# Two batches' k and v in 2304 B runs, block-diagonal exp(k), a t-outer first y and weight casts on GpSimd, in a linear-attention and GELU-MLP kernel

## The chip, the cores and the metric

The kernel runs on one core of a Trainium2 chip. The metric is the device time of one execution in microseconds (us); less is better. The kernel before takes 308.79 us (median of 3 runs, 308.36 to 309.51).

## The reference

Attention of the efficient kind (softmax of q over features, softmax of k over the sequence, then k'v, then q times that), and after it an MLP with an exact GELU. Inputs and output are float32.

```python
# q, k, v: (8 batches, 8 heads, 576, 64)
q_s = softmax(q, axis=-1)
k_s = softmax(k, axis=2)
kv  = einsum('bhsd,bhse->bhde', k_s, v)            # 64 x 64 per head
a   = einsum('bhsd,bhde->bhse', q_s, kv)
x   = a.transpose(0, 2, 1, 3).reshape(4608, 512)
out = gelu(x @ w_in) @ w_out                       # w_in 512 x 2048, w_out 2048 x 512
```

## The kernel before

Each batch of 576 rows is cut into 512 "main" rows and 64 "rest" rows; the rests of all batches are gathered into a ninth chunk. For a chunk, `h` is 16 tiles of four matmuls with a GELU on ACT behind each, and `y` is four groups (j) of 16 matmuls (t), each evacuated by DVE and stored. The attention of the next batch ("front") is woven into the matmuls. The parts that the argument touches:

```python
v_aug = [singles.tile([128, J, HP, PA], BF16, name=f"v_aug{i}") for i in range(2)]   # 4 x 4 x 130

def cast_v(b, hp):            # fp32 -> bf16, one pair of heads
    o = v_aug[b % 2][:, :, hp, :].rearrange("p j (two w) -> p two j w", two=2)
    s = st[b]["vf"].rearrange("p (x two) (j d) -> p x two j d", two=2, j=J)
    nc.vector.tensor_copy(out=o[:, :, :, 0:D], in_=s[:, hp])

def cast_v_all(b):
    cast_vr(b)                # the 64 rest rows
    for hp in range(HP):
        cast_v(b, hp)

def norm_q(b, parts=1, engs=None):       # later batches: reduce and reciprocal on DVE, multiply on GpSimd
    ...
        nc.vector.reduce_sum(out=qsum[:, :, hs], in_=eq[:, :, hs, :], axis=AX.X)
        nc.vector.reciprocal(recq[:, :, hs], qsum[:, :, hs])
        engs[i % len(engs)].tensor_tensor(out=eq[:, :, hs, :], in0=eq[:, :, hs, :], in1=..., op=ALU.mult)

def dve_front(b):
    norm_q(b)
    if b < B:
        cast_v_all(b)

def y_phase(c, ins):
    for j in range(J):
        ps = psum_y.tile([128, DM], FP32, tag="y")          # two banks in turn
        for t in range(NDF):
            nc.tensor.matmul(ps, g[:, t, j * 128:(j + 1) * 128], wo_bf[:, t, :], ...)
            for f in ins.get((j, t), []):
                f()
        y_sb = moe_sb.tile([128, DM], FP32, tag="y_sb")
        nc.vector.tensor_copy(out=y_sb, in_=ps)
        ...                                                  # store
...
for c in range(2, B + 1):
    ...
    h_phase(c, ins)                                          # c == 2: dve_front(3) in it
    if nb <= B:
        exp_q(nb) ... exp_k(nb); table(AF.Gelu)
        yi[(1, 15)] = [lambda nb=nb: dve_front(nb)]
    y_phase(c, yi)
```

The softmax here doesn't subtract the row's maximum and nothing guards it: scores larger than these inputs give would overflow.

## Time and profile before

| stage | from to (us) | length |
|---|---|---|
| start, to h of batch 0 | 0 to 21.24 | 21.24 |
| h of batch 0 | to 36.91 | 15.67 |
| y of batch 0, front of batch 1 | to 59.15 | 22.24 |
| h of batch 1 | to 74.67 | 15.52 |
| y of batch 1, front of batch 2 | to 93.16 | 18.49 |
| h of batch 2, front of batch 3 | to 109.87 | 16.71 |
| y of batch 2 | to 123.68 | 13.81 |

From there on h with a front (16.7) and y (13.8) alternate with no wait. A full group of 64 wide matmuls takes 13.81 us at full clock. A chain line has its start, its length and what ran; a timeline line adds the operation, shapes, count, and in brackets the idle time before it and what ended it.

The prediction does not show one place that later mattered: y of batch 2, on DVE and GpSimd. This is the timeline of the kernel before, of the two engines.

```profile
113.36 0.69 DVE L266 COPY y_sb<-ps 128x512 f32<-128x512 f32 x1 [2.76 <-PE ps L259]
114.08 2.29 DVE L159 TENSOR_REDUCE qsum<-e 128x32 f32<-128x2048 bf16 x1
116.40 0.35 DVE L160 RECIPROCAL recq<-qsum 128x32 f32<-128x32 f32 x1
116.67 0.36 DVE L136 CAST vr_aug<-r 64x512 bf16<-64x512 f32 x1
116.95 1.41 DVE L144 CAST v_aug<-f 128x512 bf16<-128x512 f32 x4
118.28 0.68 DVE L266 COPY y_sb<-ps 128x512 f32<-128x512 f32 x1
...
116.93 4.92 POOL L161 TENSOR_TENSOR e<-e,recq 128x2048 bf16<-128x2048 bf16 x1 [15.24 <-PE ps L259]
...
239.07 3.62 POOL L161 TENSOR_TENSOR e<-e,recq 128x2048 bf16<-128x2048 bf16 x1 [25.61 <-DVE recq L160]
```

Four casts of v follow one another every 0.35 us, the second evacuation of y comes right after them, and the GpSimd multiply (POOL), which was released at the same moment, takes 4.92 us beside them. The last line is the multiply of the ninth chunk, which has no casts of v beside it: 3.62 us.

### The profile page before, as it was taken

How to read it: one execution, taken by the hardware profiler on the slowest of the kernel's cores; microseconds unless marked ns; L12 is line 12 of the kernel's file. 1: busy time of each engine (PE TensorE's matmuls, PEld its weight loads, DVE VectorE, ACT ScalarE, POOL GpSimd, SP SyncE). 2: the span in 40 equal slices, each digit the busy share in tenths (PEclk: the TensorE clock that was granted, in tenths of full speed). 3: DMA queues.
4: the chain of work that ended last, by engine and by line, in shares of the span. 5: the costliest groups of instructions: out<-in, count | busy, mean ns of one | idle time of the engine just before them, and what ended most of it. 6: DMA issues, size and time to landing. Idle time of an engine off the chain costs nothing.

```text
span 307.6 us, 3824 instructions
## 1 busy us (share of the span) xinstructions
PE 288.6 (94%) x1541; PEld 138.4 (45%) x1541; DVE 122.0 (40%) x218; ACT 151.7 (49%) x212; POOL 38.3 (12%) x23
## 2 busy tenths in 40 slices
PE   5759998699899999999999999999999999999993
PEld 1424444244445544544454445444644455444441
DVE  4754437410777355342534344434433223110021
ACT  4546754367924582458245924591457056006400
POOL 6200002000204206000600060006000400000000
PEclk9588999699999999999999999999999999999999
DMA  7999999995026902691279117911600100110033
GB/s 219 316 381 387 369 263 304 312 304 152 2 102 190 286 23 84 188 271 51 73 207 270 37 69 213 265 36 68 153 21 34 70 34 0 36 70 33 2 68 68
DMA packets 47809, 46.38 MB, mean 151 GB/s; under 512 B 14000, under 2 KB 39600, under 8 KB 47792
## 3 DMA queue, kind: packets, MB, share of 16 engines
q1 hardware_dynamic: 47792, 46.14, 51.4%
q8 instruction: 12, 0.20, 0.3%
q14 instruction: 5, 0.04, 0.0%
HBM read 36.70 MB, written 9.44 MB: 150 GB/s over the span
## 4 chain that ended last, share of the span: by engine, by line
PE 89%; DVE 4%; ACT 3%; DMA 2%; issue 1%; POOL 1%; SPq 0%; ACTq 0%; DVEq 0%
PE ps L246 42%; PE ps L259 38%; PE ps L209 3%; PE ps L169 3%; PE ps L225 2%; DMA f<-in_q_dram 2%; ACT e L123 1%; DVE qsum L159 1%; PE ps L328 1%; DVE y_sb L266 1%; POOL e L161 1%; DVE xT L235 1%; PE ps L173 1%; DVE kvbd L197 0%; ACT L123 0%
## 5 line engine op out<-in xcount | busy, mean ns | idle before, releaser
L250 ACT ACTIVATE g<-ps 128x512 bf16<-128x512 f32 x144 | 86.0, 597 | 116.1 <-PE ps L246 116.1
L246 PE MATMUL ps<-xT,wi_bf 128*128 128x512 bf16 x576 | 136.5, 386 | 1.7 <-ACT wi_bf L294 1.7
L259 PE MATMUL ps<-wo_bf,g 128*128 128x512 bf16 x576 | 126.6, 379 | 1.2 <-DVE y_sb L266 1.2
L259 PEld LDWEIGHTS <-g 128*128 128x128 bf16 x576 | 56.3, 98 | 68.8 <-issue 1.9
L246 PEld LDWEIGHTS <-wi_bf 128*128 128x128 bf16 x576 | 55.9, 99 | 66.2 <-issue 4.7
L266 DVE COPY y_sb<-ps 128x512 f32<-128x512 f32 x36 | 24.8, 689 | 96.9 <-PE ps L259 96.9
L161 POOL TENSOR_TENSOR e<-e,recq 128x2048 bf16<-128x2048 bf16 (+1 forms) x9 | 33.9, 3765 | 203.8 <-DVE recq L160 171.4
L123 ACT ACTIVATE e<-f 128x2048 bf16<-128x2048 f32 (+1 forms) x20 | 31.2, 1563 | 7.9 <-DMA f<-in_q_dram 4.3
L235 DVE CAST xT<-ps 128x512 bf16<-128x512 f32 x32 | 21.8, 689 | 20.1 <-PE ps L225 16.8
L159 DVE TENSOR_REDUCE qsum<-e 128x16 f32<-128x1024 bf16 (+1 forms) x12 | 20.9, 1743 | 19.1 <-ACT e L123 18.9
L216 DVE COPY qT<-ps 128x1024 bf16<-128x1024 bf16 x17 | 11.6, 690 | 15.3 <-PE ps L209 15.3
L169 PE MATMUL ps<-v_aug,e 128*128 128x129 bf16 x128 | 11.7, 228 | 4.6 <-DVE v_aug L144 2.8
L209 PE MATMUL ps<-identity,e 128*128 128x128 bf16 x144 | 11.7, 229 | 4.0 <-POOL e L161 3.9
L169 PEld LDWEIGHTS <-e 128*128 128x128 bf16 x128 | 9.5, 101 | 9.9 <-DVE v_aug L144 2.6
L209 PEld LDWEIGHTS <-e 128*128 128x128 bf16 x144 | 9.9, 102 | 8.5 <-POOL e L161 5.0
L225 PE MATMUL ps<-qT,kvbd 128*128 128x512 bf16 x32 | 12.2, 401 | 1.5 <-ACT kvbd L193 1.2
L144 DVE CAST v_aug<-f 128x512 bf16<-128x512 f32 x32 | 11.7, 415 | 2.5 <-DMA f<-in_v_dram 2.5
L79 ACT ACT_TABLE_LOAD x9 | 11.5, 1283 | 0.9 <-PEq L439 0.7
L328 PE MATMUL ps<-zeros 128*128 128x512 bf16 x21 | 7.9, 528 | 1.2 <-DVE scr L69 1.2
L186 DVE RECIPROCAL rec<-ps 128x2 f32<-128x2 f32 (+1 forms) x18 | 3.0, 169 | 14.6 <-PE ps L173 14.6
L197 DVE TENSOR_TENSOR kvbd<-ps,rec 64x128 bf16<-64x128 f32 (+1 forms) x30 | 8.4, 278 | 0.9
L123 ACT ACT_TABLE_LOAD x6 | 7.7, 1283 | 0.1
(32 smaller groups left out, 63.1 us busy)
## 6 DMA issues: line engine op xcount, KB each, us to landing
out_dram<-y_sb SPq DMA_DIRECT2D x32, 256.0 KB, 2.3
f<-in_q_dram SPq DMA_DIRECT2D x6, 1024.0 KB, 7.5
f<-in_k_dram SPq DMA_DIRECT2D x6, 1024.0 KB, 10.5
f<-in_v_dram SPq DMA_DIRECT2D x6, 1024.0 KB, 10.2
w<-in_moe_w_out_dram SPq DMA_DIRECT2D x4, 1024.0 KB, 11.4
w<-in_moe_w_in_dram SPq DMA_DIRECT2D x3, 1024.0 KB, 11.1
f<-in_q_dram SPq DMA_DIRECT2D x4, 512.0 KB, 9.2
f<-in_k_dram SPq DMA_DIRECT2D x4, 512.0 KB, 8.9
```

The costliest lines, as they stand in the source:

```text
L123: nc.scalar.activation(out=dst[:, i * n:(i + 1) * n], in_=src[:, i * n:(i + 1) * n], func=AF.Exp)
L144: nc.vector.tensor_copy(out=o[:, :, :, 0:D], in_=s[:, hp])
L159: nc.vector.reduce_sum(out=qsum[:, :, hs], in_=eq[:, :, hs, :], axis=AX.X)
L161: engs[i % len(engs)].tensor_tensor(out=eq[:, :, hs, :], in0=eq[:, :, hs, :], in1=recq[:, :, hs].unsqueeze(3).to_broadcast([128, J, n, D]) ...
L169: nc.tensor.matmul(ps, st[b]["ek"][:, j, hs, :].rearrange("p h d -> p (h d)"), v_aug[b % 2][:, j, hp, 0:PW], start=(j == 0), stop=False,)
L209: nc.tensor.transpose(ps[:, j, i, :], st[b]["eq"][:, j, 2 * hp:2 * hp + 2, :].rearrange("p h d -> p (h d)"), identity,)
L225: nc.tensor.matmul(ps, kvbd[b][:, hp, :], st[b]["qT"][:, :, hp, :], start=True, stop=True)
L235: nc.vector.tensor_copy(out=st[b]["xT"][:, hp, :], in_=ps)
L246: nc.tensor.matmul(ps, wi_bf[:, dm, t * 128:(t + 1) * 128], xT[:, dm, :], start=(dm == 0), stop=(dm == NDM - 1),)
L250: nc.scalar.activation(out=g[:, t, :], in_=ps, func=AF.Gelu)
L259: nc.tensor.matmul(ps, g[:, t, j * 128:(j + 1) * 128], wo_bf[:, t, :], start=(t == 0), stop=(t == NDF - 1),)
L266: nc.vector.tensor_copy(out=y_sb, in_=ps)
```

## The change

Its intent is to shorten the start and the two transitions that are not hidden: load k and v of batches 0 and 1 in contiguous 2304 B runs (nine rows of a head per partition), use a block-diagonal exp(k) so that such runs serve as weights, cast weights on idle GpSimd, and let the first y run its first 48 matmuls over four banks before batch 1 is needed. Core of the diff, with cuts:

```diff
-    v_aug = [singles.tile([128, J, HP, PA], BF16, name=f"v_aug{i}") for i in range(2)]
+    v_flat = [singles.tile([128, HP * NS * VW], BF16, name=f"v_aug{i}") for i in range(2)]   # 4*9*66 = 2376
+    v_aug = [
+        t[:, 0:J * HP * PA].rearrange("p (j x w) -> p j x w", j=J, x=HP) for t in v_flat
+    ]
+    v_pair = [t.rearrange("p (x n w) -> p x n w", x=HP, n=NS) for t in v_flat]
...
+    def load_pair(b, name, t, parts):          # 2304 B runs
+        src = t[b].rearrange("h (p n) d -> (h p) (n d)", n=NS).rearrange("(x q) f -> q x f", q=128)
...
+    def exp_k_pair(b, half):                   # two ACT exps of 64 partitions each
...
+    def kv_pair(b, hp):                        # nine matmuls of 65 columns
...
-        for t in range(NDF):
-            ps = psum_h.tile([128, M], FP32, tag="h")
+        for t0 in [0] + list(range(group, NDF)):      # group=2: first two h tiles side by side
...
+            for h in range(2):                        # first two weight casts
+                nc.gpsimd.tensor_copy(out=o[:, 2 * h:2 * h + 2], in_=w[:, 2 * h:2 * h + 2, 0:n])
...
-    warm(12)
+    warm(24)
...
+    for t in range(12):                               # first y, over four banks
+        for j in range(J):
+            y_mm(0, yps[j], j, t)
+    norm_q(1, 0, 2)
+    norm_q(1, 1, 2)
+    cast_wo(3, wo[3])
...
+        (1, 12): [lambda: kv_step(2, (0, 1))],        # y of batch 1: finer places for batch 2's steps
+        (2, 2): [lambda: kv_step(2, (2, 3))],
...
-            yi[(1, 15)] = [lambda nb=nb: dve_front(nb)]
+            yi[(1, 0)] = [lambda nb=nb: norm_q(nb)]
+            if nb < B:
+                yi[(1, 15)] = [lambda nb=nb: cast_v_all(nb)]
```

Not shown: the v casts of batches 2 and 3 get a small memset of the ones column ahead of them. Batches 2 to 7 keep the old layout of v; for them `v_aug` is now a view into the first 2080 elements of the flat tile that batches 0 and 1 use as `v_pair`.

More of the change, by code (lines that the diff above doesn't have):

```diff
@@ L41 @@
     PA = 2 * D + 2
+    NS = S // 64
+    VW = D + 2
     singles = ctx.enter_context(tc.tile_pool(name="singles", bufs=1))
@@ L59 @@
     wo_bf = singles.tile([128, NDF, DM], BF16)
-    v_aug = [singles.tile([128, J, HP, PA], BF16, name=f"v_aug{i}") for i in range(2)]
+    v_flat = [singles.tile([128, HP * NS * VW], BF16, name=f"v_aug{i}") for i in range(2)]
[3 more added lines that the diff above has]
+    v_pair = [t.rearrange("p (x n w) -> p x n w", x=HP, n=NS) for t in v_flat]
+    ek_flat = [singles.tile([128, 2 * NS * 128], BF16, name=f"ek{i}") for i in range(2)]
+    ek_main = [
+        t[:, 0:J * H * D].rearrange("p (j h d) -> p j h d", j=J, h=H) for t in ek_flat
+    ]
+    ek_pair = [t.rearrange("p (x n m) -> p x n m", x=2, n=NS) for t in ek_flat]
     vr_aug = [singles.tile([128, HP, PA], BF16, name=f"vr_aug{i}") for i in range(2)]
@@ L70, in setup_tiles @@
         for i in range(2):
-            nc.vector.memset(v_aug[i][:, :, :, D:D + 1], 1.0)
+            nc.vector.memset(v_pair[i][:, :, :, D:D + 1], 1.0)
+            nc.vector.memset(ek_pair[i][0:64, :, :, 64:128], 0.0)
+            nc.vector.memset(ek_pair[i][64:128, :, :, 0:64], 0.0)
             nc.vector.memset(vr_aug[i][0:R, :, D:D + 1], 1.0)
@@ L74, in setup_tiles @@
             nc.vector.memset(ek_r[i][R:128], 0.0)
-        for b in range(B):
+        for b in range(B - 1):
             nc.gpsimd.memset(kvbd[b], 0.0)
@@ L81, with load_main @@
     st = [dict() for _ in range(B + 1)]
-    def load_main(b, name, t, eng, parts=1):
-        f = f32in.tile([128, H, J * D], FP32, tag=name + "f")
+    def load_main(b, name, t, parts=1):
+        f = f32in.tile([128, 2048 if name == "q" else 2560], FP32, tag=name + "f")
+        f = f[:, 0:2048].rearrange("p (h f) -> p h f", h=H)
         st[b][name + "f"] = f
@@ L88, in load_main, with load_both, load @@
         for i in range(parts):
-            eng.dma_start(out=f[:, i * n:(i + 1) * n, :], in_=src[:, i * n:(i + 1) * n, :])
-    def load_rest(b, name, t, eng):
-        r = f32in.tile([R, H, D], FP32, tag=name + "r")
-        st[b][name + "r"] = r
-        eng.dma_start(out=r, in_=t[b, :, M:S, :].rearrange("h p d -> p h d"))
-    def load(b, qp=1, kp=1, vp=1, keng=None):
-        keng = keng or nc.sync
-        load_main(b, "q", q, nc.sync, qp)
-        load_rest(b, "k", k, keng)
-        load_main(b, "k", k, keng, kp)
-        load_rest(b, "v", v, nc.sync)
-        load_main(b, "v", v, nc.sync, vp)
+            nc.sync.dma_start(out=f[:, i * n:(i + 1) * n, :], in_=src[:, i * n:(i + 1) * n, :])
+    def load_pair(b, name, t, parts):
+        f = f32in.tile([128, 2560], FP32, tag=name + "f")
+        f = f[:, 0:HP * NS * D].rearrange("p (x f) -> p x f", x=HP)
+        st[b][name + "f"] = f
+        src = t[b].rearrange("h (p n) d -> (h p) (n d)", n=NS).rearrange("(x q) f -> q x f", q=128)
+        n = HP // parts
+        for i in range(parts):
+            nc.sync.dma_start(out=f[:, i * n:(i + 1) * n, :], in_=src[:, i * n:(i + 1) * n, :])
+    def load_both(b, name, t):
+        f = f32in.tile([128, 2560], FP32, tag=name + "f")
+        r = f[0:R, 2048:2560].rearrange("p (h d) -> p h d", h=H)
+        f = f[:, 0:2048].rearrange("p (h f) -> p h f", h=H)
+        st[b][name + "f"], st[b][name + "r"] = f, r
+        nc.sync.dma_start(out=r, in_=t[b, :, M:S, :].rearrange("h p d -> p h d"))
+        nc.sync.dma_start(out=f, in_=t[b, :, 0:M, :].rearrange("h (p j) d -> p h (j d)", j=J))
+    def load(b):
+        load_main(b, "q", q)
+        load_both(b, "k", k)
+        load_both(b, "v", v)
     def load_qrest():
-        f = f32in.tile([128, J, H, D], FP32, tag="qf")
+        f = f32in.tile([128, 2048], FP32, tag="qf")
+        f = f.rearrange("p (j h d) -> p j h d", j=J, h=H)
         st[B]["qf"] = f
@@ L113, in exp_main @@
     def exp_main(b, name, parts=1):
-        e = attn_sb.tile([128, J, H, D], BF16, tag="e" + name)
+        if name == "q":
+            e = attn_sb.tile([128, J, H, D], BF16, tag="eq")
+        else:
+            e = ek_main[b % 2]
         st[b]["e" + name] = e
@@ L132, in exp_k, with cast_v_pair, norm_pair @@
         exp_main(b, "k", parts)
+    def exp_k_pair(b, half):
+        src = st[b]["kf"].rearrange("p x (n d) -> p x n d", n=NS)
+        for hh in range(2):
+            pr = slice(hh * 64, hh * 64 + 64)
+            nc.scalar.activation(
+                out=ek_pair[half][pr, :, :, hh * 64:hh * 64 + 64],
+                in_=src[pr, 2 * half:2 * half + 2], func=AF.Exp,
+            )
+    def cast_v_pair(b, hp, eng):
+        eng.tensor_copy(
+            out=v_pair[b][:, hp, :, 0:D],
+            in_=st[b]["vf"][:, hp, :].rearrange("p (n d) -> p n d", n=NS),
+        )
+    def kv_pair(b, hp):
+        ps = psum_a.tile([128, 512], FP32, tag="a")
+        st[b][f"kvp{hp}"] = ps
+        for n in range(NS):
+            nc.tensor.matmul(
+                ps[:, 0:D + 1], ek_pair[hp // 2][:, hp % 2, n, :], v_pair[b][:, hp, n, 0:D + 1],
+                start=(n == 0), stop=(n == NS - 1),
+            )
+    def norm_pair(b, hp, eng1):
+        ps = st[b][f"kvp{hp}"]
+        rec = small.tile([128, 2], FP32, tag="reck")
+        nc.vector.reciprocal(rec[:, 0:1], ps[:, D:D + 1])
+        for hh in range(2):
+            pr = slice(hh * 64, hh * 64 + 64)
+            dst = kvbd[b][pr, hp, hh * 64:hh * 64 + 64]
+            if hh == 1 and eng1 == "s":
+                nc.scalar.activation(out=dst, in_=ps[pr, 0:D], func=AF.Copy, scale=rec[pr, 0:1])
+            else:
+                nc.vector.tensor_scalar_mul(out=dst, in0=ps[pr, 0:D], scalar1=rec[pr, 0:1])
     def cast_vr(b):
@@ L146, in cast_v_all @@
     def cast_v_all(b):
+        if b < 4:
+            nc.vector.memset(v_aug[b % 2][:, :, :, D:D + 1], 1.0)
         cast_vr(b)
@@ L149, in cast_v_all, with norm_q @@
             cast_v(b, hp)
-    def norm_q(b, parts=1, engs=None):
-        engs = engs or [nc.gpsimd]
+    def norm_q(b, i=0, n=1, eng=None):
+        eng = eng or nc.gpsimd
         eq = st[b]["eq"]
-        qsum = small.tile([128, J, H], FP32, tag="qsum")
-        recq = small.tile([128, J, H], FP32, tag="recq")
-        n = H // parts
-        for i in range(parts):
-            hs = slice(i * n, (i + 1) * n)
-            nc.vector.reduce_sum(out=qsum[:, :, hs], in_=eq[:, :, hs, :], axis=AX.X)
-            nc.vector.reciprocal(recq[:, :, hs], qsum[:, :, hs])
-            engs[i % len(engs)].tensor_tensor(
-                out=eq[:, :, hs, :], in0=eq[:, :, hs, :],
-                in1=recq[:, :, hs].unsqueeze(3).to_broadcast([128, J, n, D]), op=ALU.mult,
-            )
+        w = H // n
+        hs = slice(i * w, (i + 1) * w)
+        qsum = small.tile([128, J, w], FP32, tag="qsum")
+        recq = small.tile([128, J, w], FP32, tag="recq")
+        nc.vector.reduce_sum(out=qsum, in_=eq[:, :, hs, :], axis=AX.X)
+        nc.vector.reciprocal(recq, qsum)
+        eng.tensor_tensor(
+            out=eq[:, :, hs, :], in0=eq[:, :, hs, :],
+            in1=recq.unsqueeze(3).to_broadcast([128, J, w, D]), op=ALU.mult,
+        )
     def kv_mm(b, ps, hp):
@@ L176, in kv_mm, with kv_step @@
         )
-    def kv_step(b, hps, split=False):
+    def kv_step(b, hps):
         n = len(hps)
@@ L190, in kv_step, with tp_mm @@
             dst = kvbd[b][pr, hx, hh * 64:hh * 64 + 64]
-            if split and hh == 1:
-                for i in range(n):
-                    nc.scalar.activation(
-                        out=dst[:, i], in_=src[:, i], func=AF.Copy, scale=rec[pr, i:i + 1]
-                    )
-            else:
-                nc.vector.tensor_tensor(
-                    out=dst, in0=src, in1=rec[pr, 0:n].unsqueeze(2).to_broadcast([64, n, D]),
-                    op=ALU.mult,
-                )
-    def tp_step(b, half, eng="v"):
+            nc.vector.tensor_tensor(
+                out=dst, in0=src, in1=rec[pr, 0:n].unsqueeze(2).to_broadcast([64, n, D]),
+                op=ALU.mult,
+            )
+    def tp_mm(b, half):
         if half == 0:
@@ L205, in tp_step @@
         ps = psum_a.tile([128, J, 2, 128], BF16, tag="a")
+        st[b][f"tp{half}"] = ps
         for i in range(2):
@@ L213, in tp_step, with tp_evac, x_mm @@
                 )
-        o = st[b]["qT"][:, :, 2 * half:2 * half + 2, :]
-        if eng == "v":
-            nc.vector.tensor_copy(out=o, in_=ps)
-        else:
-            nc.scalar.copy(out=o, in_=ps)
+    def tp_evac(b, half):
+        nc.vector.tensor_copy(
+            out=st[b]["qT"][:, :, 2 * half:2 * half + 2, :], in_=st[b][f"tp{half}"]
+        )
+    def tp_step(b, half):
+        tp_mm(b, half)
+        tp_evac(b, half)
     def x_step(b, hp, eng="v"):
+        x_mm(b, hp)
+        x_evac(b, hp, eng)
+    def x_mm(b, hp):
         if hp == 0:
@@ L223, in x_step @@
         ps = psum_a.tile([128, M], FP32, tag="a")
+        st[b][f"x{hp}"] = ps
         if b < B:
@@ L233, in x_step, with x_evac @@
                 )
+    def x_evac(b, hp, eng="v"):
+        ps = st[b][f"x{hp}"]
         if eng == "v":
@@ L237, in x_step, with h_phase @@
             nc.scalar.copy(out=st[b]["xT"][:, hp, :], in_=ps)
-    def h_phase(c, ins):
+    def h_phase(c, ins, group=1):
         g = moe_sb.tile([128, NDF, M], BF16, tag="g", bufs=1)
@@ L242, in h_phase, with y_mm, y_out @@
         xT = st[c]["xT"]
-        for t in range(NDF):
-            ps = psum_h.tile([128, M], FP32, tag="h")
+        for t0 in [0] + list(range(group, NDF)):
+            ts = range(t0, t0 + (group if t0 == 0 else 1))
+            pss = [psum_h.tile([128, M], FP32, tag="h", name="ps") for t in ts]
             for dm in range(NDM):
-                nc.tensor.matmul(
-                    ps, wi_bf[:, dm, t * 128:(t + 1) * 128], xT[:, dm, :],
-                    start=(dm == 0), stop=(dm == NDM - 1),
-                )
-            nc.scalar.activation(out=g[:, t, :], in_=ps, func=AF.Gelu)
-            for f in ins.get(t, []):
-                f()
+                for ps, t in zip(pss, ts):
+                    nc.tensor.matmul(
+                        ps, wi_bf[:, dm, t * 128:(t + 1) * 128], xT[:, dm, :],
+                        start=(dm == 0), stop=(dm == NDM - 1),
+                    )
+            for ps, t in zip(pss, ts):
+                nc.scalar.activation(out=g[:, t, :], in_=ps, func=AF.Gelu)
+                for f in ins.get(t, []):
+                    f()
+    def y_mm(c, ps, j, t):
+        nc.tensor.matmul(
+            ps, st[c]["g"][:, t, j * 128:(j + 1) * 128], wo_bf[:, t, :],
+            start=(t == 0), stop=(t == NDF - 1),
+        )
+    def y_out(c, ps, j):
+        y_sb = moe_sb.tile([128, DM], FP32, tag="y_sb")
+        last = c == B and j == J - 1
+        if last:
+            nc.vector.tensor_copy(out=y_sb[:, 0:DM // 2], in_=ps[:, 0:DM // 2])
+            nc.scalar.copy(out=y_sb[:, DM // 2:DM], in_=ps[:, DM // 2:DM])
+        else:
+            nc.vector.tensor_copy(out=y_sb, in_=ps)
+        if c < B:
+            dst = out[c * S:c * S + M, :].rearrange("(p j) n -> p j n", j=J)[:, j, :]
+            nc.sync.dma_start(out=dst, in_=y_sb)
+        else:
+            for b2 in range(2):
+                r0 = (2 * j + b2) * S + M
+                eng = nc.scalar if last and b2 == 1 else nc.sync
+                eng.dma_start(out=out[r0:r0 + R, :], in_=y_sb[b2 * R:(b2 + 1) * R, :])
     def y_phase(c, ins):
-        g = st[c]["g"]
         for j in range(J):
@@ L258, in y_phase @@
             for t in range(NDF):
-                nc.tensor.matmul(
-                    ps, g[:, t, j * 128:(j + 1) * 128], wo_bf[:, t, :],
-                    start=(t == 0), stop=(t == NDF - 1),
-                )
+                y_mm(c, ps, j, t)
                 for f in ins.get((j, t), []):
                     f()
-            y_sb = moe_sb.tile([128, DM], FP32, tag="y_sb")
-            nc.vector.tensor_copy(out=y_sb, in_=ps)
-            if c < B:
-                dst = out[c * S:c * S + M, :].rearrange("(p j) n -> p j n", j=J)[:, j, :]
-                nc.sync.dma_start(out=dst, in_=y_sb)
-            else:
-                for b2 in range(2):
-                    r0 = (2 * j + b2) * S + M
-                    nc.sync.dma_start(out=out[r0:r0 + R, :], in_=y_sb[b2 * R:(b2 + 1) * R, :])
+            y_out(c, ps, j)
     wi_cols = [256, 256, 512, 512, 512]
@@ L290, in cast_wi @@
         o = wi_bf[:, :, wi_off[i]:wi_off[i] + n]
-        if eng == "v":
+        if eng == "p":
+            for h in range(2):
+                nc.gpsimd.tensor_copy(out=o[:, 2 * h:2 * h + 2], in_=w[:, 2 * h:2 * h + 2, 0:n])
+        else:
             nc.vector.tensor_copy(out=o, in_=w[:, :, 0:n])
-        else:
-            nc.scalar.copy(out=o, in_=w[:, :, 0:n])
     def load_wo(i):
@@ L304, in cast_wo @@
         nc.vector.tensor_copy(out=wo_bf[:, 4 * i:4 * i + 4, :], in_=w)
-    def kv_chain(b, warm=lambda n: None):
-        cast_vr(b)
-        cast_v(b, 0)
-        cast_v(b, 1)
-        kv_step(b, (0, 1), split=True)
-        warm(2)
-        cast_v(b, 2)
-        kv_step(b, (2,), split=True)
-        x_step(b, 0)
-        x_step(b, 1, "s")
-        warm(2)
-        cast_v(b, 3)
-        kv_step(b, (3,), split=True)
-        x_step(b, 2)
-        x_step(b, 3, "s")
-    zeros = singles.tile([128, 512], BF16)
+    zeros = kvbd[B - 1].rearrange("p x m -> p (x m)")
     def warm(n):
@@ L328, in warm @@
             nc.tensor.matmul(ps, zeros[:, 0:128], zeros, start=True, stop=True)
-    load(0, qp=2, kp=2, vp=4)
+    load_main(0, "q", q, 2)
+    load_pair(0, "k", k, 2)
+    load_pair(0, "v", v, 4)
     wi = [load_wi(i) for i in range(5)]
-    wo = [load_wo(i) for i in range(4)]
-    load(1, qp=2, kp=2, vp=4)
+    wo = [load_wo(i) for i in range(3)]
+    load_main(1, "q", q, 2)
+    wo.append(load_wo(3))
+    load_pair(1, "k", k, 2)
+    load_pair(1, "v", v, 4)
     load(2)
@@ L337 @@
     setup_tiles()
-    warm(12)
+    warm(24)
     table(AF.Exp)
     exp_q(0, parts=2)
-    exp_k(0, parts=2)
-    table(AF.Gelu)
-    norm_q(0, parts=2, engs=[nc.gpsimd, nc.vector])
-    tp_step(0, 0)
-    tp_step(0, 1)
-    warm(5)
-    kv_chain(0, warm)
-    cast_wi(0, wi[0], "s")
-    cast_wi(1, wi[1], "v")
+    exp_k_pair(0, 0)
+    exp_k_pair(0, 1)
+    norm_q(0, 0, 2)
+    norm_q(0, 1, 2)
+    tp_step(0, 0)
+    cast_v_pair(0, 0, nc.vector)
+    cast_v_pair(0, 1, nc.gpsimd)
+    kv_pair(0, 0)
+    tp_mm(0, 1)
+    norm_pair(0, 0, "s")
+    table(AF.Gelu)
+    cast_v_pair(0, 2, nc.vector)
+    tp_evac(0, 1)
+    kv_pair(0, 1)
+    warm(2)
+    norm_pair(0, 1, "s")
+    x_step(0, 0)
+    cast_v_pair(0, 3, nc.gpsimd)
+    kv_pair(0, 2)
+    norm_pair(0, 2, "s")
+    x_step(0, 1, "s")
+    kv_pair(0, 3)
+    norm_pair(0, 3, "s")
+    x_step(0, 2)
+    x_step(0, 3, "s")
+    cast_wi(0, wi[0], "p")
+    cast_wi(1, wi[1], "p")
     cast_wi(2, wi[2], "v")
@@ L355 @@
         12: [lambda: cast_wo(1, wo[1])],
-    })
+    }, group=2)
     exp_q(1, parts=2)
-    exp_k(1, parts=2)
+    exp_k_pair(1, 0)
+    exp_k_pair(1, 1)
     table(AF.Gelu)
     cast_wo(2, wo[2])
-    cast_wo(3, wo[3])
-    y_phase(0, {
-        (2, 0): [lambda: norm_q(1, parts=2, engs=[nc.gpsimd, nc.vector])],
-        (3, 3): [lambda: tp_step(1, 0)],
-        (3, 7): [lambda: tp_step(1, 1, "s")],
-    })
-    kv_chain(1)
-    h_phase(1, {12: [lambda: cast_v_all(2)]})
+    yps = [psum_h.tile([128, DM], FP32, tag="h", name="ps") for j in range(2)]
@@ new lines @@
+    yps += [psum_y.tile([128, DM], FP32, tag="y", name="ps") for j in range(2)]
+    for t in range(12):
[3 more added lines that the diff above has]
+    norm_q(1, 1, 2)
+    cast_wo(3, wo[3])
+    tp_step(1, 0)
+    for t in range(12, NDF):
+        y_mm(0, yps[0], 0, t)
+    y_out(0, yps[0], 0)
+    for t in range(12, NDF):
+        y_mm(0, yps[1], 1, t)
+    tp_step(1, 1)
+    y_out(0, yps[1], 1)
+    for t in range(12, NDF):
+        y_mm(0, yps[2], 2, t)
@@ new lines @@
+    cast_v_pair(1, 0, nc.gpsimd)
+    cast_v_pair(1, 1, nc.vector)
+    kv_pair(1, 0)
+    norm_pair(1, 0, "v")
+    for t in range(12, NDF):
+        y_mm(0, yps[3], 3, t)
+    kv_pair(1, 1)
+    x_step(1, 0)
+    cast_v_pair(1, 2, nc.gpsimd)
+    norm_pair(1, 1, "v")
+    cast_v_pair(1, 3, nc.vector)
+    kv_pair(1, 2)
+    x_step(1, 1, "s")
+    norm_pair(1, 2, "v")
+    kv_pair(1, 3)
+    norm_pair(1, 3, "v")
+    x_step(1, 2)
+    x_step(1, 3, "s")
+    y_out(0, yps[2], 2)
+    y_out(0, yps[3], 3)
@@ L372 @@
+    h_phase(1, {12: [lambda: cast_v_all(2)]}, group=2)
     load(3)
-    exp_q(2)
+    exp_q(2, parts=2)
     exp_k(2)
-    def front3():
-        exp_q(3)
-        exp_k(3)
-        table(AF.Gelu)
-    front3()
-    y_phase(1, {
-        (0, 15): [lambda: norm_q(2, parts=2, engs=[nc.gpsimd, nc.vector])],
-        (1, 15): [lambda: kv_step(2, (0, 1)), lambda: kv_step(2, (2, 3))],
-        (2, 7): [lambda: tp_step(2, 0), lambda: tp_step(2, 1)],
-        (3, 3): [lambda hp=hp: x_step(2, hp, "v") for hp in range(HP)],
+    exp_q(3)
@@ L387 @@
+    exp_k(3)
+    table(AF.Gelu)
+    y_phase(1, {
+        (0, 15): [lambda: norm_q(2, 0, 2)],
+        (1, 1): [lambda: norm_q(2, 1, 2, nc.vector)],
+        (1, 12): [lambda: kv_step(2, (0, 1))],
+        (2, 2): [lambda: kv_step(2, (2, 3))],
+        (2, 4): [lambda: tp_step(2, 0)],
+        (2, 6): [lambda: tp_step(2, 1)],
+        (3, 0): [lambda: x_step(2, 0)],
+        (3, 4): [lambda: x_step(2, 1)],
+        (3, 8): [lambda: x_step(2, 2)],
+        (3, 12): [lambda: x_step(2, 3)],
     })
```

## The prediction

> **What bounds the kernel now.** I read the page's header and its 40 slices first, then the chain that ended last in order of time, to see where the tensor engine (PE) is not in its steady rhythm; then busy time by stage; then the timeline of the stages that the change touches. PE is busy for 94% of the span, so the share alone says little. The slices say where it is not at full rate:
>
> ```profile
> PE   5759998699899999999999999999999999999993
> PEclk9588999699999999999999999999999999999999
> DMA  7999999995026902691279117911600100110033
> ```
>
> One slice is 7.69 us. PE has gaps in slices 0 to 2, around 7 and at 10. The granted clock is low in slices 1 to 3 and at 7. DMA is saturated for the first nine slices and not later. From slice 12 on there is nothing to win: the chain shows each group of 64 wide matmuls at 13.81 us, with no wait until the last copy.
>
> ```profile
> 0.00:21.24 21.24, 12.35 (x62) 6.05 (x62) 12.79 (x32) 11.17 (x16) 6.33 (x15) 0.84 0.97 298
> 21.24:36.91 15.67, 15.67 (x65) 6.77 (x66) 6.64 (x6) 8.96 (x15) 0.00 (x0) 0.89 1.05 383
> 36.91:59.15 22.24, 18.42 (x106) 8.82 (x104) 13.47 (x25) 10.83 (x15) 1.90 (x1) 0.92 1.13 288
> 59.15:74.67 15.52, 15.52 (x66) 6.63 (x64) 1.51 (x5) 9.54 (x17) 0.00 (x0) 0.90 0.99 281
> ```
>
> These are stages: window and its length, busy time of PE, weight loads, DVE, ACT, POOL, then granted clock, DMA share and GB/s. The two h stages (second and fourth line) cost 15.67 and 15.52 us instead of 13.81 and show a clock near 0.9: each starts cold. The third line is y of batch 0 with the front of batch 1: 22.24 us.
>
> The chain shows what the head of the program hangs on:
>
> ```profile
> 16.74 0.59 DVE xT L235
> 17.34 0.35 DVE v_aug L144
> ...
> 18.43 0.23 DVE kvbd L197
> ...
> 18.74 0.32 ACT kvbd L193
> ...
> 19.10 0.40 PE ps L225
> ...
> 19.53 0.58 ACT xT L237
> ...
> 20.14 1.05 ACT wi_bf L294
> ...
> 21.24 3.02 PE ps L246 x7
> ```
>
> Columns are start, us, what. DVE casts, reciprocals and scalings alternate with short PE pieces, and the weight cast on ACT comes last: 1.7 us between the last xT matmul (19.5) and h. The same ladder stands between y and h of batch 1 (51.73 to 59.15). Before y of batch 1 ends there is one more hole:
>
> ```profile
> 78.52 1.23 DVE qsum L159
> ...
> 80.02 1.09 DVE qsum L159
> ...
> 81.56 1.54 issue
> 83.10 0.69 DVE y_sb L266
> ...
> 83.83 1.89 PE ps L259 x8
> ```
>
> The evacuation of y stands behind both reductions and a multiply on DVE; PE waits 1.16 us for it.
>
> **What the Trainium skill says.** (1) "TensorE: Matmul & The Clock Gate", Part 1, What's actually happening: after about one idle window of 3.4 us PE runs at half clock, and needs a busy window to recover. The trace agrees: the first four h matmuls take 1.71 us instead of 0.86, until about 25.0, 3.8 us after 21.24. (2) "SBUF — State Buffer", Who interferes with whom: DVE casts in a two-port mode, and DVE operations with two SBUF inputs against a reading GpSimd operation, exclude GpSimd for a whole instruction. It fits: the DVE multiply of 1024 elements takes 1.41 to 1.72 us when it starts under a POOL multiply, against 1.22 for the DVE reduction of the same size. (3) "ScalarE: Activation LUTs", What ACT_TABLE_LOAD costs: 186 ns plus 0.833 ns per element. The trace has 1056 ns for 1024 elements and 618 for 512, on 64 partitions: elements per partition count, so half the partitions save nothing. (4) "DMA: Bandwidth & Descriptors", Specifications: at least 512 B for line rate. The trace is stricter: weights in 2 KB runs land 1.05 MB every 2.71 us (387 GB/s; casts start at 20.51, 23.22, 25.93), q halves in 1 KB runs 0.52 MB in 1.69 us (310), and the 256 B rest of k 0.13 MB in about 1.46 us (90).
>
> **The change part by part.**
>
> *k and v in 2304 B runs.* I take 387 GB/s for them. q still lands at 6.4. Then k halves (0.59 MB, 1.52 us each) at 7.9 and 9.4, v quarters (0.76 us) at 10.2, 10.9, 11.7, 12.5, where before k ended at 11.0 and the second v quarter came at 13.3. All later loads move up by about 2 us; batch 1's q moves another 2.7 ahead of one weight load.
>
> *Block-diagonal exp(k).* Four ACT exps of 1152 elements (186 + 960 = 1.15 us, about 1.06 apart), against 0.63 + 2 x 1.06 = 2.75: about 1.5 us more ACT work per batch. Ready at 10.1 (first half) and 12.2 (second), against 12.08 before, so nothing is lost at the end and the first half comes 2 us earlier. On PE nine matmuls of 65 columns replace five of 129 per pair; the trace's 0.057 us per kv matmul warm, 0.107 cold, is the weight load's pace, so 0.51 against 0.29: +0.9 us warm per batch.
>
> *Start to h of batch 0.* Transposes at 9.4 as before (POOL multiply 7.43 to 9.33). The second multiply moves from DVE to POOL, 9.33 to 11.23. The first DVE v cast is ready to go at 10.7 but shares the port with it, so it ends at 11.7. kv 0 at 11.75 to 12.8, cold; norm to 13.75 (DVE, then ACT, as in the chain); the table load then holds ACT to 15.2; second transposes to 13.6, kv 1 to 14.6, its norm ends on ACT at 15.6. x0 at 15.2, kv 2, x1 at 16.0, kv 3 at 16.3 to 16.75, norm 2 to 17.05, x2 at 17.1, xT1 on ACT to 17.6, norm 3 to 17.9, x3 at 17.95. h begins at 18.2, against 21.24. Side by side, h has six matmuls (1.3 us) before it needs xT3 (18.85), so that copy is hidden. The weight casts on POOL (four pieces of 512 elements; the trace has no such POOL copy; my estimate is 0.7 us each from its two-input 1.9 us per 1024) run from about 14.4 to 17.8: off the path. Saved: 3.0 us.
>
> *Clock in h of batch 0.* PE now works without a long pause from 11.75 on. If it stays warm, h takes 13.81: 1.86 saved. I give that 65%: 1.2 us.
>
> *y of batch 0 and front of batch 1.* With h starting at 18.2, y starts at 32.0. t outer: 48 matmuls, 10.4 us, to 42.4, which need neither wo 3 nor batch 1. wo 3 lands near 38.5; its cast waits for the POOL multiplies (to 40.5) and ends at 41.7: just in time. Then transposes 0.45, two y (0.86 each), transposes, y, kv 0 (0.5), y: 47.4. What is left is a DVE ladder: kvbd 0 at 47.7, xT0 to 48.9, norm 1 to 49.6, v cast to 50.05, norm 2 to 50.75, norm 3 to 51.5, then x3 and h at 51.75. So 19.75 us from h to h, against 22.24: 2.5 saved. The second h probably still starts cold: PE does about 1.9 us in 3.4 before it; I put 40% on warm, worth 1.7: 0.7.
>
> *y of batch 1.* PE now does 13.81 + kv 1.15 + transposes 0.89 + x 0.88 = 16.7 against 18.49 (74.67 to 93.16): the y evacuation no longer stands behind both reductions. Taken as 1.6.
>
> *End.* The last copy is split (0.69 to about 0.42) and one of two stores is issued from ACT. After the copy ends at 303.56 the program runs 4.0 us more, for two issues in a row and a landing of 2.3. Estimate 0.6.
>
> Sum: 3.0 + 1.2 + 2.5 + 0.7 + 1.6 + 0.6 = 9.6. A schedule laid by hand has no slips; I take 0.6 off for those: 9.0 us, 308.8 to 299.8 us.
>
> **Rivals.** (a) Clock: the gain in PE's order is real, but both h stages start cold; then 1.9 of the sum goes: 301.7. For: both did before, and the gate's window is not tied to the program. Against: the long gap before h (18.4 to 21.2) goes. If both stay warm: 298. (b) The shared port and the single ACT become the bound of the start: POOL now has multiplies, v casts and weight casts, and ACT's 4.3 us of exp plus a table load lie between the norms. If POOL's copies take 1.5 us instead of 0.7, or DVE and POOL block each other at each cast, h starts at 20 or so: 301.5 to 302.5. For: 1.41 and 1.72 us for a 1.22 us operation. (c) Nothing is gained from the loads by themselves, because after 12.5 the ladder and not the data sets the pace; then undoing the run length alone would cost 1 to 2 us, at the start only. (d) t outer stalls for wo 3 or for g; slack is only 0.7 us, so a stall of 1 to 2 us is possible: 301.5.
>
> **Range and chances.** The warm-warm case with no slip gives 296.8; cold-cold with one of (b) or (d) gives 303.2. That is my 8 in 10. Two per cent faster is 302.6: it needs 6.2 of my 9.0 us. I put 0.82 on faster, 0.17 on same and 0.01 on slower.
>
> **What would show it.** h of batch 0 starts at 18.2 (within 1), lasts about 13.8 if warm; y's first 48 matmuls have no gap; h of batch 1 starts near 52; the 1.16 us hole in y of batch 1 is gone; from h of batch 2 on each stage is as before. POOL copies over 1.2 us, DVE casts of 576 elements far over 0.46 us, or a clock near 0.9 in both h stages would make it wrong.

## The result, and the profile after

Median 321.23 us (319.89 to 322.09, 4 runs) against 308.69 (308.36 to 309.51, 4 runs). The ratio is 1.0398, 95% interval 1.0354 to 1.0443: slower. A ratio here is the mean time of one kernel's fast runs over that of the other's fast runs of the same rounds, so it is not quite the ratio of the medians.

The page's slices of the changed kernel (one slice is 7.97 us):

```profile
PE   8599997999959969999799969996999999999994
PEclk9799997999989997999799979999999999999999
```

The start is fuller than before and its clock higher. But PE has new dips at slices 11, 14, 19, 23 and 27, where the kernel before showed nines, and the clock dips at or just after four of them (11, 15, 19, 23). The stages of the changed kernel, as windows (columns as in the prediction; two of the stages are told in the text only):

```profile
0.00:17.33 17.33, 12.05 (x83) 6.50 (x84) 12.23 (x32) 11.55 (x15) 11.41 (x21) 0.90 0.91 316
17.33:31.14 13.81, 13.81 (x65) 6.24 (x64) 5.59 (x5) 9.43 (x16) 0.00 (x0) 1.00 1.04 385
...
67.10:84.10 17.00, 16.93 (x106) 8.61 (x105) 11.35 (x21) 11.81 (x11) 1.90 (x1) 1.00 0.24 82
84.10:106.04 21.94, 18.26 (x105) 9.54 (x104) 13.53 (x21) 9.13 (x16) 3.98 (x1) 0.92 0.64 168
106.04:124.17 18.13, 15.66 (x66) 6.70 (x64) 10.40 (x11) 7.42 (x7) 3.91 (x1) 0.91 0.12 44
```

The first five stages came out much as predicted: h of batch 0 starts at 17.33 instead of 21.24 (saved 3.91) and is warm (13.81, saved 1.86); the next stage takes 20.45 against 22.24 (1.79); h of batch 1 is cold as before (15.51, clock 0.89); y of batch 1 takes 17.00 against 18.49 (1.49). With 0.34 at the end (4.39 us from the last matmul to the end, against 4.73) that is 9.4 us saved. Then it is lost: h of batch 2 takes 5.23 more, and y of batches 2 to 5 take 4.32, 4.39, 4.08 and 2.70 more. That is 20.7 us, and 20.7 less 9.4 is the 11.3 us by which the span grew (318.9 against 307.6).

The chain of the changed kernel shows y of batch 2:

```profile
112.58 0.35 DVE recq L228
112.93 0.28 DVE vr_aug L202
113.20 0.34 DVE v_aug L210
113.57 3.73 DVE v_aug L210
117.33 0.44 DVE v_aug L210
118.13 0.69 DVE y_sb L345
118.87 5.30 PE ps L333 x16
```

and the timeline of the changed kernel has GpSimd beside it, and PE:

```profile
113.10 3.91 POOL L229 TENSOR_TENSOR e<-e,recq 128x2048 bf16<-128x2048 bf16 x1 [21.40 <-PE ps L333]
...
118.87 5.30 PE L333 MATMUL ps<-wo_bf,g 128*128 128x512 bf16 x16 [2.46 <-DVE y_sb L345]
```

DVE does the same instructions in the same order as before, and the multiply starts at the same point (0.17 us after the reciprocal's end, 0.18 before). But the second v cast takes 3.73 us instead of 0.41 and ends at 117.30, 0.29 us after the multiply; the multiply takes 3.91 instead of 4.92. The second evacuation of y stands behind the casts, so the fourth y group waits 2.46 us for its bank, and then its 16 matmuls take 5.30 us instead of 3.45 (a quarter of 13.81) because PE went cold: the granted clock from 118.87 to 124.17 is 0.68. Of the 4.3 us, 2.5 are wait and 1.85 clock.

The list of DVE's instructions in the two built programs (not a profile) shows the one difference at that place. Before, and then after:

```
108 L144 TensorCopy v_aug0_91<-f_877 128x2x4x64 x3
114 L210 TensorCopy v_aug0_91<-f_916 128x2x4x64 [waits DVE_49] x3
```

In the changed program the second to fourth v cast of batches 2 to 6 each wait on DVE's own semaphore, that is for DVE's previous instruction to be complete (in batches 2 and 3 the first one too, behind its memset). Below this is called a self-wait.

### The profile page after: what moved, and what is told of

The parts are those of the page before. It is cut to its first block, busy times and chain, and to the rows that moved or that the text cites. A ratio compares the mean times of both kernels' runs of the same rounds, so it can differ in the third digit from the quotient of the medians.

```text
span 318.9 us, 3908 instructions
## 1 busy us (share of the span) xinstructions
PE 292.7 (92%) x1578; PEld 140.2 (44%) x1578; DVE 140.2 (44%) x224; ACT 152.9 (48%) x210; POOL 42.6 (13%) x32
## 4 chain that ended last, share of the span: by engine, by line
PE 76%; DVE 18%; issue 2%; ACT 2%; POOL 1%; DVEq 0%; ACTq 0%; POOLq 0%
PE ps L323 38%; PE ps L333 30%; DVE v_aug L210 7%; DVE qsum L227 4%; PE ps L272 3%; DVE y_sb L345 2%; PE ps L296 2%; PE ps L237 2%; DVE kvbd L198 1%; DVE v_aug L174 1%; POOL e L229 1%; ACT ek L152 1%; DVE recq L228 1%; PE ps L241 0%; DVE qT L279 0%
## 5 line engine op out<-in xcount | busy, mean ns | idle before, releaser
L333 PE MATMUL ps<-wo_bf,g 128*128 128x512 bf16 x576 | 133.0, 389 | 10.0 <-DVE y_sb L345 10.0
L345 DVE COPY y_sb<-ps 128x512 f32<-128x512 f32 x35 | 23.6, 686 | 88.4 <-PE ps L333 88.4
L309 DVE CAST xT<-ps 128x512 bf16<-128x512 f32 x32 | 22.1, 691 | 21.6 <-PE ps L296 18.2
L210 DVE CAST v_aug<-f 128x512 bf16<-128x512 f32 x24 | 26.7, 1112 | 3.1 <-DMA f<-in_v_dram 2.4
L279 DVE COPY qT<-ps 128x1024 bf16<-128x1024 bf16 x18 | 12.4, 691 | 18.4 <-PE ps L272 18.2
L152 ACT ACTIVATE e<-f 128x1024 bf16<-128x1024 f32 (+1 forms) x11 | 15.8, 1442 | 4.8 <-DMA f<-in_q_dram 4.7
L272 PEld LDWEIGHTS <-e 128*128 128x128 bf16 x144 | 9.8, 101 | 5.7 <-POOL e L229 2.0
L237 PE MATMUL ps<-v_aug,ek 128*128 128x129 bf16 x96 | 8.9, 229 | 3.7 <-DVE v_aug L210 3.7
L168 ACT ACTIVATE ek<-f 64x1152 bf16<-64x1152 f32 x8 | 9.3, 1162 | 4.4 <-DMA f<-in_k_dram 4.3
L152 ACT ACTIVATE ek<-f 128x2048 bf16<-128x2048 f32 x6 | 11.4, 1894 | 0.0
L237 PEld LDWEIGHTS <-ek 128*128 128x128 bf16 x96 | 7.4, 103 | 7.3 <-issue 4.4
L401 PE MATMUL ps<-kvbd 128*128 128x512 bf16 x26 | 7.7, 457 | 1.2 <-DVE scr L82 1.2
```

The source lines that it names most:

```text
L152: nc.scalar.activation(out=dst[:, i * n:(i + 1) * n], in_=src[:, i * n:(i + 1) * n], func=AF.Exp)
L237: nc.tensor.matmul(ps, st[b]["ek"][:, j, hs, :].rearrange("p h d -> p (h d)"), v_aug[b % 2][:, j, hp, 0:PW], start=(j == 0), stop=False,)
L272: nc.tensor.transpose(ps[:, j, i, :], st[b]["eq"][:, j, 2 * hp:2 * hp + 2, :].rearrange("p h d -> p (h d)"), identity,)
L309: nc.vector.tensor_copy(out=st[b]["xT"][:, hp, :], in_=ps)
L333: nc.tensor.matmul(ps, st[c]["g"][:, t, j * 128:(j + 1) * 128], wo_bf[:, t, :], start=(t == 0), stop=(t == NDF - 1),)
```

## The experiments

Theory A: these self-waits open a gap between casts, GpSimd takes the port that it shares with DVE (point 2 of the prediction's skill section) in the gap, and keeps it for its whole multiply. Theory B: the multiply was moved from j=1, t=15 to j=1, t=0 and so starts too early. Other rivals: the longer runs, the t-outer y or the GpSimd weight casts. Four kernels told these apart on one chip, beside 7 runs of the kernel before (median 309.23).

**e1, no self-waits.** Same tile to within 24 elements, same schedule:

```diff
-    v_flat = [singles.tile([128, HP * NS * VW], BF16, name=f"v_aug{i}") for i in range(2)]
-    v_aug = [
-        t[:, 0:J * HP * PA].rearrange("p (j x w) -> p j x w", j=J, x=HP) for t in v_flat
-    ]
+    v_nat = [singles.tile([128, J, HP, 150], BF16, name=f"v_aug{i}") for i in range(2)]
+    v_aug = [t[:, :, :, 0:PA] for t in v_nat]
+    v_flat = [t.rearrange("p j x w -> p (j x w)")[:, 0:HP * NS * VW] for t in v_nat]
```

> The changed kernel with one edit: the shared v tile is declared as 4 x 4 x 150 instead of as 2376 flat elements, and batches 2 to 6 take a native slice of it. The schedule of every engine stays, but the second to fourth v cast of a batch no longer wait on DVE's own semaphore. Theory A (the self-waits leave gaps in which GpSimd takes the shared port and holds it for 3.9 us, while y's evacuation stands behind the casts on DVE): each y stage falls from 16.5 to 18.2 back to 13.8 us, h of batch 2 from 21.9 to 16.7, the GpSimd multiply lengthens from 3.91 to about 4.9 us, and the time falls from 321.2 by about 20 to 300 to 302. Theory B (the multiply's place at j=1, t=0 instead of t=15 starts it too early): no change, 320 to 322.

Measured: 300.39 us (299.05 to 300.79), ratio 0.9716 (0.9693 to 0.9738). The whole loss is gone. The timeline of e1 in y of batch 2:

```profile
106.91 1.42 DVE L211 CAST v_aug<-f 128x512 bf16<-128x512 f32 x4
108.25 0.67 DVE L346 COPY y_sb<-ps 128x512 f32<-128x512 f32 x1
...
106.88 4.92 POOL L230 TENSOR_TENSOR e<-e,recq 128x2048 bf16<-128x2048 bf16 x1 [15.10 <-PE ps L334]
```

The four casts take 1.42 us together, and now GpSimd pays: 4.92 against 3.91, as before the change. The multiply is still at j=1, t=0, so theory B is out already.

**e2, the multiply's place back.**

```diff
-            yi[(1, 0)] = [lambda nb=nb: norm_q(nb)]
-            if nb < B:
-                yi[(1, 15)] = [lambda nb=nb: cast_v_all(nb)]
+            yi[(1, 15)] = [lambda nb=nb: dve_front(nb)]
```

> The changed kernel with the normalisation of later batches moved back to where it stood before (after the last matmul of j=1), self-waits kept. Theory A: no change, 319 to 322, because the multiply started 0.18 us after the reciprocal in both kernels. Theory B: the loss goes, 300 to 304.

Measured: 320.83 us (319.87 to 323.29), ratio 1.0384 (1.0338 to 1.0431): nothing changed. Theory B is out from the other side too.

**e3, the self-waits alone, in the kernel before.**

```diff
-    v_aug = [singles.tile([128, J, HP, PA], BF16, name=f"v_aug{i}") for i in range(2)]
+    v_flat = [singles.tile([128, HP * 9 * 66], BF16, name=f"v_aug{i}") for i in range(2)]
+    v_aug = [
+        t[:, 0:J * HP * PA].rearrange("p (j x w) -> p j x w", j=J, x=HP) for t in v_flat
+    ]
```

> The kernel before with one edit: its v tile becomes a slice of a flat tile of 2376 elements, which puts the same self-waits on the v casts of batches 2 to 6 and changes nothing else. Theory A: 4 to 5 us more in each of five stages, 325 to 330. Theory B, or any theory that blames the longer DMA runs, the t-outer y or the weight casts: 308 to 310, as before.

Measured: 329.31 us (328.57 to 330.11), ratio 1.0647 (1.0619 to 1.0675), 20.1 us more. The timeline of e3 has the changed kernel's picture, with nothing else of the change in it:

```profile
122.54 5.09 DVE L147 CAST v_aug<-f 128x512 bf16<-128x512 f32 x4
...
122.52 3.91 POOL L164 TENSOR_TENSOR e<-e,recq 128x2048 bf16<-128x2048 bf16 x1 [21.61 <-PE ps L262]
...
128.28 3.61 PE L262 MATMUL ps<-wo_bf,g 128*128 128x512 bf16 x16 [2.46 <-DVE y_sb L269]
```

The edit also puts one self-wait on the second v cast of batches 0 and 1. That matters little: h of batch 2 and y of batches 2 to 5 hold 19.2 of the 19.4 us by which the profiled span grew (327.0 against 307.6).

So the declaration of one tile is worth 20 us in either kernel, and the rest of the change is worth about 9.

**e4, self-waits kept, multiply out of the way.** In the changed kernel the casts stand ahead of the reduction on DVE, so that no multiply can run beside them:

```diff
-            yi[(1, 0)] = [lambda nb=nb: norm_q(nb)]
-            if nb < B:
-                yi[(1, 15)] = [lambda nb=nb: cast_v_all(nb)]
+            yi[(1, 0)] = [lambda nb=nb: dve_front(nb)]
     def dve_front(b):
-        norm_q(b)
         if b < B:
             cast_v_all(b)
+        norm_q(b)
```

> The changed kernel with the self-waits kept, but on DVE the v casts of batches 3 to 6 stand ahead of the reduction and reciprocal that release the GpSimd multiply, so that no multiply can run beside them. Theory A: casts of 0.41 to 0.45 us, y stages of 13.8, 300 to 303. If the self-waits cost the time by themselves and not through the port, the loss stays nearly whole: 317 or more.

Measured: 302.17 us (301.10 to 303.22), ratio 0.9769 (0.9731 to 0.9807). The timeline of e4:

```profile
106.42 1.80 DVE L210 CAST v_aug<-f 128x512 bf16<-128x512 f32 x4
108.14 2.28 DVE L227 TENSOR_REDUCE qsum<-e 128x32 f32<-128x2048 bf16 x1
...
110.97 3.62 POOL L229 TENSOR_TENSOR e<-e,recq 128x2048 bf16<-128x2048 bf16 x1 [17.14 <-DVE recq L228]
```

A self-wait by itself costs about 0.1 us per waiting cast (four casts, three of them waiting, in 1.80 instead of 1.42); it is the multiply in the gap that costs 3.3. Run alone, the multiply takes 3.62. The 1.8 us that e4 stands above e1 were not taken apart by a run. Its chain shows two likely parts: the transposes of batch 3 now wait for the later multiply (which ends at 93.85, while h of batch 2 began about 9 us earlier; that stage takes 17.38 us, 16.71 in e1), and h of batch 1 is cold in the profiled run (15.51 us), where e1's was warm (13.83).

Next, the parts of the 9 us, each undone on top of e1 (three kernels, and a fourth that adds to e1, on another chip; before 309.31, 11 runs). e1 is compared by the ratios to the kernel before.

**f1, j outer.** The first y with j outer and the fourth wo load ahead of batch 1's q:

```diff
-    for t in range(12):
-        for j in range(J):
-            y_mm(0, yps[j], j, t)
+    cast_wo(3, wo[3])
+    for t in range(NDF):
+        y_mm(0, yps[0], 0, t)
+    y_out(0, yps[0], 0)
...
```

> On top of e1 (300.4): the first y again with j outer, and the fourth wo load again ahead of batch 1's q. If t outer is what lets y start early without wo 3: wo 3 lands near 35.5 us and is cast by 36.8, while j outer needs it at 34.5, so PE waits about 2.3 us and may go cold for another 1.7: 302.5 to 304.5. If t outer is only a reordering: 300 to 301.

Measured: 302.18 us (300.55 to 305.39), ratio 0.976 (0.9722 to 0.9797). That is about 1.4 us above e1's ratio, but the intervals overlap. The profiled run is slow (305.39, over 1.5% above the fastest), so its waits of 1.27 and 1.71 us for the wo casts are only a hint. Inconclusive: t outer is worth something like 1 us, less than I expected.

**f2, half the run length.**

```diff
+            for c in range(2):
                 nc.sync.dma_start(
-                    out=f[:, i * n:(i + 1) * n, :], in_=src[:, i * n:(i + 1) * n, :])
+                    out=f[:, i * n:(i + 1) * n, c * hw:(c + 1) * hw],
+                    in_=src[:, i * n:(i + 1) * n, c * hw:(c + 1) * hw])
```

> On top of e1: each k and v load of batches 0 and 1 is issued as two with runs of 1152 B, all else equal. If the run length matters: k and v of batch 0 land 0.7 to 1.2 us later and h of batch 0 starts that much later, 301 to 302. If it is hidden (rival c of the prediction): within 0.5 of e1.

Measured: 300.79 us (299.36 to 303.97), ratio 0.9723 (0.9693 to 0.9753): as e1. In its trace the first v cast starts at 10.56 and waits for no load; the last v quarter is there at 13.02, between the 12.65 and 13.38 of two profiles of e1. Runs of 1152 B do as well as 2304 B here; the prediction's rival (c) holds at that step. (Runs of 256 B, which the new layout also removes, were not tried.)

**f3, weight casts back on ACT and DVE.**

```diff
-    cast_wi(0, wi[0], "p")
-    cast_wi(1, wi[1], "p")
+    cast_wi(0, wi[0], "s")
+    cast_wi(1, wi[1], "v")
```

> On top of e1: the first two weight casts back on ACT and DVE, at the end of the start's ladder. If moving them to GpSimd took 1.0 us off the path: 301 to 302, and up to 303.5 if PE also goes cold before h. If they are hidden: within 0.5 of e1.

Measured: 303.88 us (303.57 to 304.77), ratio 0.9832 (0.9806 to 0.9857), 3.5 us more than e1. The windows of h of batch 0 in f3:

```profile
18.96:34.48 15.52, 15.46 (x64) 6.78 (x66) 6.80 (x6) 8.85 (x15) 0.00 (x0) 0.90 1.06 380
```

h starts at 18.96, behind an ACT cast of 1.05 us, and it starts cold (15.52 us, clock 0.90). In two profiles of e1 it started at 18.09 and 17.50 and took 13.81. So 0.9 to 1.5 us of delay come with another 1.7 us of clock.

**g1, a better version.** All v casts of batch 1 on GpSimd (idle there), and six matmuls on zeros in PE's waits before h of batch 1:

```diff
-    cast_v_pair(1, 1, nc.vector)
+    cast_v_pair(1, 1, nc.gpsimd)
-    cast_v_pair(1, 3, nc.vector)
+    cast_v_pair(1, 3, nc.gpsimd)
     kv_pair(1, 2)
+    warm(3, psum_h)
     x_step(1, 1, "s")
...
+    warm(1, psum_h)
     x_step(1, 2)
+    warm(2, psum_h)
     x_step(1, 3, "s")
```

> On top of e1: all four v casts of batch 1 on GpSimd, and six matmuls on zeros in the waits of the ladder before h of batch 1. If the DVE ladder sets that stage's end: h of batch 1 starts 1 to 1.5 us earlier and always warm, 297.5 to 299.5. If something else does: as e1, 299 to 301.

Measured: 298.13 us (297.13 to 300.02), ratio 0.9648 (0.9611 to 0.9685): the lowest median here. Its interval lies below that of e1's first call, but overlaps that of e1's second call below, and the two parts of the edit were not run apart. Windows of g1 (h of batch 0, y of batch 0 with the front of batch 1, h of batch 1):

```profile
17.40:32.63 15.23, 15.18 (x64) 6.57 (x64) 6.13 (x5) 9.43 (x16) 0.00 (x0) 0.91 1.05 383
32.63:51.64 19.01, 18.22 (x124) 9.18 (x126) 12.33 (x24) 10.72 (x11) 7.40 (x6) 1.00 1.10 337
51.64:65.40 13.76, 13.71 (x64) 6.27 (x64) 3.40 (x9) 9.43 (x16) 0.00 (x0) 1.00 1.11 305
```

The transition is 19.01 us, against 20.46 in both profiles of e1, and h of batch 1 is warm; that it always is, as expected, is not shown, for it was warm in one of e1's profiles too (13.83 us, and 15.51 in the other). In this execution h of batch 0 happened to start cold, though all edits of g1 lie after it: such 1.4 to 1.7 us come and go between runs of one kernel.

Last, e1 again as a base and three small parts (a third call; before 309.38, 11 runs).

**e1 again.**

> e1 once more, as the base on this chip: 299 to 301.5, in two groups 1.7 us apart as PE starts an h stage warm or cold.

Measured: 299.86 us (298.50 to 302.63), ratio 0.9699 (0.9651 to 0.9748).

**f4, one h tile at a time** (`group=1` in both places).

> On top of e1: the first h tiles one after the other again. In e1 the last xT copy ends 0.63 us after h begins, just when a lone first tile would need it: within 0.5 of e1. If side by side hid more: 0.6 to 1.2 more than e1.

Measured: 300.11 us (299.54 to 302.57), ratio 0.9703 (0.9668 to 0.9738): no difference seen. Side by side hides nothing that was not hidden already.

**f5, coarse places in y of batch 1** (the four places of the kernel before).

> On top of e1: in y of batch 1 the steps of batch 2 back in the four coarse places of the kernel before. If the finer places remove the 1.16 us hole before the third y and the wait at the x steps: 1.2 to 1.7 us more than e1, 301 to 302.5. If the hole goes anyway: as e1.

Measured: 301.77 us (299.73 to 303.05), ratio 0.9742 (0.9706 to 0.9779): 1.3 us above e1 by ratio, with overlapping intervals. The chain of f5 has the old hole again:

```profile
72.11 1.64 issue
73.75 0.69 DVE y_sb L346
...
74.48 1.89 PE ps L334 x8
```

The stage is 17.65 us long here (66.17 to 83.82) and 16.93 in the profile of e1 again (67.28 to 84.21). So in the profiles the finer places are worth 0.7 us in this stage, with the hole as their visible cause; in the whole time the gain is not clear of noise.

**f6, 12 warm-up matmuls** instead of 24.

> On top of e1: 12 warm-up matmuls at the start instead of 24. The first transposes start cold (0.45 us more), but the first v quarter lands about 11 us and comes after them: within 0.5 of e1, unless the longer idle time changes the clock of h of batch 0, then up to 1.9 more.

Measured: 300.40 us (298.91 to 302.76), ratio 0.9701 (0.9664 to 0.9739): no difference seen.

## Why the prediction was wrong

**The step that failed** is the sentence "From slice 12 on there is nothing to win", with its counterpart at the end, "from h of batch 2 on each stage is as before". I took it that stages whose instructions stay the same keep their time. DVE's order there did stay the same, but three waits were added, by the way one tile is declared. What the runs showed in its place: +20.7 us in five stages of the changed kernel, 20 us in e3 by that declaration alone, and none of it in e1. It was not the early place of the multiply (e2), nor the self-waits by themselves (e4).

**The mechanism was at hand.** The prediction quotes the Trainium skill on the shared port and names it in rival (b), but only for the start. It also lies in the trace before: the multiply took 4.92 us beside the casts there, against 3.62 alone (239.07). That difference was the sign that two engines met there in every batch, and that it was DVE's unbroken run of casts that decided it. I saw the longer multiply and did not ask what would happen if the winner changed.

**The steps that held.** Start: h at 17.33 (predicted 18.2). Clock: warm, 1.86. Transition: h of batch 1 at 51.59 (51.75). Cold start of that h: as the likelier case. y of batch 1: 17.0 (16.7). End: 0.34 (0.6). Together 9.4 us, against 9.6; e1, the change without its flaw, runs at 300.4 and 299.9, against 299.8 predicted. That the sums agree so closely is partly luck: the start saved 0.9 us and the clock of h of batch 0 0.7 us more than their terms, the transition and the clock of h of batch 1 0.7 us each less.

**Right sums with wrong terms.** The first DVE v cast was to wait for the multiply and end at 11.7; it was not blocked and ended at 11.30 in the changed kernel, but took 0.74 us instead of 0.46. GpSimd's copy of 512 elements took 0.62 us (0.7). Longer runs were credited with the early loads; f2 shows no gain from the length beyond 1152 B. The weight casts on GpSimd were told as a part of the start's 3.0 us; they turned out to be the largest part that was tested, 3.5 us with the clock that comes with them (f3). Two readings of the prediction do not hold. Its 310 GB/s for 1 KB runs of q come from a start in which the 256 B rest of k is next in the queue; in the changed kernel and in e1 the same two halves land 1.42 to 1.48 us apart, 354 to 369 GB/s. And its warm-warm case with no slip comes to 297.5 by its own terms, not 296.8.

**Open:** why the program gets the self-waits. A flat tile of exactly 2080 elements, built but not run, has none; a slice of 2080 out of 2376 has them. That the tracking of overlaps fails on a view which does not fill its tile fits this, but was only argued. Also open is why y of batch 5 lost 2.70 and not 4.3: its wait is the same, but PE stayed warm, and what decides that between runs was not tested; in e2 and e3 y of batches 2 and 4 stayed warm instead (16.4 to 16.5 us), so it is not tied to the batch. And no run undid the new layout of k and v as a whole (the block-diagonal exp(k), and no 256 B rests), so its share of the start is not shown.

## What to carry to other kernels

A diff of a schedule is not only the order of instructions but also their waits: compare the lists of waits wherever a tile's declaration or view changed, even for stages that the change does not mean to touch. Where DVE casts and GpSimd arithmetic run side by side, find out which of them wins today and by what; an order that holds only because DVE leaves no gap is fragile, and an evacuation that PE needs should not stand behind it. A delay before a long matmul stage can cost twice, once as a wait and once as clock (here 2.46 and 1.85 us).

## What the Trainium skill lacked or had wrong

- "SBUF — State Buffer", Who interferes with whom, says that whoever issues first gets the shared pair for the whole instruction. The runs agree, and add what it does not say: a run of DVE casts back to back (1.42 us for four in e1) holds GpSimd's multiply up throughout (4.92 us against 3.62 alone), although the multiply is released before the second one; one wait on DVE's own semaphore, a gap of 0.03 us in the chain (113.54 to 113.57), is enough for the multiply to come first and the next cast to take 3.73 us.
- "Advanced Engine Details and Errata", VectorE Performance Modes, 2x-2p Requirements: no point against it. It asks for a most non-unit major dimension that is even in source and destination, or odd and equal in both. In the built program the DVE cast of nine rows of 64 (fp32 to bf16, both in SBUF) has a source of one run of 576 and a destination of 9 x 64, which is neither. It took 0.73 to 0.75 us, against 0.41 for 512 elements in even dimensions; and a first one at 10.56 ran beside a GpSimd multiply without being held up.
- "DMA: Bandwidth & Descriptors", Specifications, names 512 B for line rate: no point against it. Runs of 1152 B did as well as 2304 B in f2 (ratio 0.9723 against 0.9716); the 256 B rest of k, which the prediction read at about 90 GB/s, lies below that size.
- "TensorE: Matmul & The Clock Gate", Part 1: no point against it. The variation that it warns of is in the runs: h of batch 1 took 13.83 us in one profile of e1 and 15.51 in another, and h of batch 0 took 13.81 us in the changed kernel and 15.23 in g1, with a start at the same 17.3 to 17.4 us.
